# Mask products on strips of 32 rows in a clustered attention with token mixing

## The chip, the cores and the metric

The kernel runs on one core of a Trainium2 chip. The metric is the device time of one execution in microseconds, as the median of several runs of the same program; each run starts from inputs in the chip's memory and ends when the output lies there. Before the change the median of 3 runs is 792.83 us.

## The reference

Four batches, eight heads, 768 tokens and 64 channels a head. Each token of q and of k is assigned to one of 16 clusters of its head, and a query attends only to keys of its own cluster. The output of the attention goes through a token mixing stage, which the change does not touch.

```
q_assign = argmax(einsum('bhsd,hcd->bhsc', q_n, c_n)); k_assign = the same of k_n
mask   = q_assign[..., :, None] == k_assign[..., None, :]
scores = where(mask, (q @ k.T) / sqrt(D), -1e9)
attn   = softmax(scores);  x = attn @ v          # heads side by side: x is (4, 768, 512)
theta  = x @ w_theta;  zr, zi = x * cos(theta), x * sin(theta)
u      = x + w_tok_r @ zr + w_tok_i @ zi
out    = u + max(u @ w_ch, 0)
```

## The kernel before, in words

Work goes by pairs of heads: 4 batches x 4 pairs = 16 pairs. A head has 64 channels, so head j = 0 or 1 of a pair lies in rows 64j to 64j+63 of the tiles, and its products use that half of TensorE's 128 rows. Two products of different halves can run side by side; a pair of them is called a slot here.

The mask is a product too. `mk` and `mq` (128 x 768) hold per half 16 rows of one-hot cluster numbers; mk holds -2^60 wherever the key is *not* in the row's cluster. The product over these rows adds a huge negative number to a score where the clusters differ. One further row per half (row 64j+32) is 1 in mk and carries in mq the negated row maximum of a query, so that the same product also subtracts the maximum.

There are two passes over the scores, which share TensorE in the loop over units at the end of the attention part:

- *Maxima.* `max_products(u, j)` makes, for one tile of 128 queries and head j, two banks `m` of 384 keys each: a product of the high parts (hq, hk) and the mask product (mq, mk), four in all. VectorE reduces both banks to a maximum, `nm` (line 396). `shift_row` transposes the maxima (`mt`, line 404), and two DMAs (line 417) write them into the row of mq.
- *Scores.* `score_products(u, j)` makes, for 128 keys by 384 queries, one bank `sc` out of four products: hk.hq, hk.lq, lk.hq and mk.mq. ScalarE takes the exponential (`at`, line 437), GpSimd adds them up (`acc`, line 448), and `weighted` multiplies them by the values (`av`, line 509: 128 rows by 64 columns, the two heads in the two halves of the columns).

There are 192 units (16 pairs, two halves of the queries, six blocks of keys). The loop takes two units a round. The maxima run LEAD = 10 units ahead of the scores, one query tile of both heads a round. So five rounds do maxima alone, then 91 rounds do both, then five do scores alone. A round that does both issues on TensorE, in this order: scores of unit u of both heads; scores of unit u+1, head 0, beside the maxima of head 1 (`scores_beside_max`); the value products of two earlier units; scores of u+1, head 1, beside the maxima of head 0. In time, three groups of products (a head's score beside the other's maxima, both heads' scores, a head's score beside the other's maxima) therefore lie between two sets of value products. `interleave` issues the products of such a group alternately, a slot at a time. Between the groups small pieces of the next pair are put in: the assignment to clusters (`lg`, `lt`, `rt`), transposes of maxima (`mt`), sums (`sm`).

`in_order` chains the instructions of each engine in the order in which the code wrote them, so TensorE's order is that of the code. The `m` banks are four of the eight banks (two tiles of two), scores and small pieces share three, `av` has one.

The one-hot rows come about in two ways. For pair 0, `assign` compares cluster numbers with a row of 16 numbers (line 291) and transposes the result on TensorE (`ot`, line 298). For the other fifteen pairs, the cluster numbers are written to memory (`rd`) and broadcast to 16 rows per head and operand by four DMAs of 48 KB (line 326) on the SP queue; the comparison with the row number then makes mq and mk. Constants by row are `mcl` (the row's cluster number), `ncl` and `mbi` (the factor of mk by row).

Of the kernel before, what the change touches and what calls it, by code (L numbers as in the profile page):

```python
# [2 lines left out]

# [11 lines left out]
ALU = mybir.AluOpType  # L15
# [26 lines left out]
def kernel(  # L42
# [19 lines left out]
    nc = tc.nc  # L62
    B, H, D, S = qT.shape
    P = 128
    NP = H // 2
    NT = S // P
    C = cent.shape[0] // H
    DM = w_theta.shape[0]
    NCT = DM // P
    HS = S // 2  # L70
# [22 lines left out]

    mbi = cpool.tile([P, 1], F32, name="mbi")
    nc.vector.memset(mbi, 0.0)
    for r in (0, 64):
        nc.vector.memset(mbi[r:r + C], -BIG)
        nc.vector.memset(mbi[r + 32:r + 33], 1.0)

    mci = cpool.tile([P, 1], I32, name="mci")  # L100
    for r in (0, 64):
        nc.gpsimd.iota(mci[r:r + 64], pattern=[[0, 1]], base=C, channel_multiplier=-1)
    mcl = cpool.tile([P, 1], F32, name="mcl")
    nc.vector.tensor_copy(out=mcl, in_=mci)
    ncl = cpool.tile([P, 1], F32, name="ncl")
# [81 lines left out]
    for x in range(3):  # L187
        x = (NPAIR + x) % 3
# [7 lines left out]
    def m_tile(name):  # L196
        return ps0.tile([P, 2, 512], F32, tag="m", name=name)

    def bank(name):
        return ps.tile([P, 512], F32, tag="bank", name=name)  # L200
# [36 lines left out]
    def f(ap):  # L237
        return ap.bitcast(F32)

    NG = HS // C  # L240

    cl = {n: pe.tile([P, S], F32, name=f"cl{n}") for n in "qk"}

    ohp = cl["q"].bitcast(BF16).rearrange("p (n t j c) -> p n t j c", n=2, j=2, c=64)
    nc.vector.memset(ohp, 0.0)
    nc.gpsimd.memset(cl["k"], -100.0)
    wb = wc.unsqueeze(1).broadcast_to([P, NG, C])
    def assign(pi):

        b, p = divmod(pi, NP)
        raws = []
        for n, src, eng in (("q", qT, nc.sync), ("k", kT, nc.scalar if pi == 0 else nc.sync)):
            raw = pw.tile([P, S], F32, tag="raw", name=f"raw{n}{pi}", bufs=3)
            st.setdefault(pi, dict(tsets[pi % 3]))["raw" + n] = raw
            eng.dma_start(out=raw, in_=src[b, 2 * p:2 * p + 2].rearrange("h d s -> (h d) s"))
            raws.append(raw)
        yield
        lg = bank(f"lg{pi}")[:, 0:HS]  # L260
        for g in range(4):
            a, n = divmod(g, 2)
            nc.tensor.matmul(  # L263
                lg[32 * g:32 * g + 32], lhsT=cb[:, p, :, :],
                rhs=raws[n][:, a * HS:(a + 1) * HS], start=True, stop=True)
        lgs = pe.tile([P, HS], F32, tag="lgs", name=f"lgs{pi}")
        nc.scalar.copy(out=lgs, in_=lg)
        yield

        lt = (m_tile(f"lt{pi}")[:, 0] if pi > 1 else bank(f"lt{pi}"))[:, 0:HS]  # L270
        ltp = lt.rearrange("p (g a t c) -> p a g t c", a=2, t=NH, c=C)
        for t in range(HS // P):
            sl = slice(t * P, (t + 1) * P)

            nc.tensor.transpose(out=ltp[:, :, :, t], in_=lgs[:, sl], identity=identf)  # L275
        ltv = lt.rearrange("p (g c) -> p g c", c=C)
        mx = pe.tile([P, NG], F32, tag="mxl", name=f"mxl{pi}")
        nc.vector.tensor_reduce(out=mx, in_=ltv, op=ALU.max, axis=AX.X)
        eq = pe.tile([P, NG, C], BF16, tag="eq", name=f"eq{pi}")
        nc.vector.tensor_tensor(  # L280
            out=eq, in0=ltv, in1=mx.unsqueeze(2).broadcast_to([P, NG, C]), op=ALU.is_equal)
        yield

        nc.vector.tensor_tensor(out=eq, in0=eq, in1=wb, op=ALU.mult)
        rr = pe.tile([P, NG], F32, tag="rr", name=f"rr{pi}")
        nc.vector.tensor_reduce(out=rr, in_=eq, op=ALU.max, axis=AX.X)
        if pi == 0:

            keep_up(4 * WARM)
            for n in range(2):  # L290
                nc.vector.tensor_tensor(
                    out=ohp[:, n, :, :, 0:C].rearrange("p t j c -> p j t c"),
                    in0=wb.rearrange("p (n j t) c -> p n j t c", n=2, j=2)[:, n],
                    in1=rr.unsqueeze(2).broadcast_to([P, NG, C]).rearrange(
                        "p (n j t) c -> p n j t c", n=2, j=2)[:, n], op=ALU.is_equal)
                ot = bank(f"ot{n}").bitcast(BF16)[:, 0:S]
                for t in range(NT):
                    nc.tensor.transpose(
                        out=ot[:, t * P:(t + 1) * P], in_=ohp[:, n, t].rearrange("p j c -> p (j c)"), identity=identb)
                if n == 0:  # L300
                    nc.scalar.copy(out=st[pi]["mq"], in_=ot)
                else:
                    nc.vector.tensor_scalar(  # L303
                        out=st[pi]["mk"], in0=ot, scalar1=BIG, scalar2=mbi, op0=ALU.mult, op1=ALU.add)
            nc.gpsimd.memset(cl["q"], -100.0)
            return
        yield

        if "mt" in st.get(pi - 2, {}):
            mt = st[pi - 2].pop("mt")  # L310
            rt = mt[0:NG, P:2 * P]
            nc.tensor.transpose(out=rt, in_=rr, identity=identf)
            shift_out(pi - 2, 1, mt)
        else:
            rt = bank(f"rt{pi}")[0:NG, 0:P]
            nc.tensor.transpose(out=rt, in_=rr, identity=identf)
        ri = pe.tile([NG, P], F32, tag="ri", name=f"ri{pi}")
        nc.scalar.copy(out=ri, in_=rt)
        yield
        rd = dram.tile([NG, P], F32, tag="rd", name=f"rd{pi}", bufs=2)  # L320
        nc.sync.dma_start(out=rd, in_=ri)
        yield
        rv = rd.rearrange("(g t) x -> g (t x)", t=NT)
        for n, x in enumerate("qk"):
            for j in range(2):
                nc.sync.dma_start(
                    out=cl[x][64 * j:64 * j + C], in_=rv[2 * n + j:2 * n + j + 1].broadcast_to([C, S]))
        yield

        mq = st[pi]["mq"]  # L330
        if pi == 1:

            nc.gpsimd.tensor_scalar(out=mq, in0=cl["q"], scalar1=mcl, scalar2=None, op0=ALU.is_equal)
        else:
            nc.scalar.activation(out=mq, in_=cl["q"], func=AF.Abs, bias=ncl)
            yield
            nc.scalar.activation(out=mq, in_=mq, func=AF.Relu, scale=-1.0, bias=1.0)
        yield
        nc.vector.tensor_scalar(
            out=st[pi]["mk"], in0=cl["k"], scalar1=mcl, scalar2=mbi, op0=ALU.not_equal, op1=ALU.mult)  # L340
# [27 lines left out]

    def interleave(*lists):

        for x in zip(*lists):
            for j, (out, stat, cols, mov, over, start, stop) in x:
                r = slice(64 * j, 64 * j + 64)
                nc.tensor.matmul(out, lhsT=stat[r, cols], rhs=mov[r, over], start=start, stop=stop)  # L374

    def max_products(u, j):

        pi, a, i = split_u(u)
        s = st[pi]
        if i == 0 and ("nm", a) not in s:  # L380
            s["nm", a] = p2.tile([P, 2, NH], F32, tag="nm", name=f"nm{u}")
        t = a * NH + i // 2
        m = s["m", j] = m_tile(f"m{u}_{j}")
        q = slice(t * P, (t + 1) * P)
        res = []
        for c in range(2):
            k = slice(c * HS, (c + 1) * HS)
            res.append((j, (m[:, c, 0:HS], s["hq"], q, s["hk"], k, True, False)))
            res.append((j, (m[:, c, 0:HS], s["mq"], q, s["mk"], k, False, True)))
        return res  # L390

    def max_of(u, j):
# [19 lines left out]
    def shift_out(pi, a, mt):  # L412
        s = st[pi]
        mr = p2.tile([NT, P], F32R, tag="mr", name=f"mr{pi}{a}")
        nc.scalar.copy(out=mr, in_=mt[0:NT, 0:P])
        for j in range(2):
            nc.sync.dma_start(
                out=f(s["mq"][64 * j + 32:64 * j + 33, a * HS:(a + 1) * HS]).rearrange("o (t n) -> o t n", n=P),
                in_=f(mr[j * NH:(j + 1) * NH]))

    def score_products(u, j, banks=None):

        pi, a, i = split_u(u)
        s = st[pi]
        if ("at", a, i) not in s:
            s["at", a, i] = p3.tile([P, 2, HS], F32, tag="at", name=f"at{u}", bufs=NAT)
        sc = banks[:, j] if banks else ps.tile([P, 512], F32, tag="bank", name=f"sc{u}_{j}")
        sc = s["sc", j] = sc[:, 0:HS]
        k, q = slice(i * P, (i + 1) * P), slice(a * HS, (a + 1) * HS)
        parts = (("hk", "hq"), ("hk", "lq"), ("lk", "hq"), ("mk", "mq"))  # L430
        return [(j, (sc, s[x], k, s[z], q, n == 0, n == 3)) for n, (x, z) in enumerate(parts)]

    def exps(u, j):

# [236 lines left out]
    start = len(nc.cur_bb.bb.instructions)  # L671
# [30 lines left out]
    while u <= NUT or todo:  # L702
        start = len(nc.cur_bb.bb.instructions)
# [303 lines left out]
```

## Time and profile before

| | |
|---|---|
| median of 3 runs | 792.83 us (792.48 to 794.13) |
| profiled execution | 792.87 us, span 791.1 us, TensorE clock 0.991 |
| TensorE busy | 774.3 us, 98% of the span |
| VectorE, ScalarE, GpSimd busy | 572.6, 386.5, 488.3 us |
| maxima, first to last product | 14.8 to 421.8 us |
| scores, first to last product | 31.3 to 446.9 us |

Times in the profile are microseconds from the start of the span; PE is TensorE's products, PEld its weight loads, DVE VectorE, ACT ScalarE, POOL GpSimd, SPq the queue that issues DMAs. A timeline row gives start, duration, engine, line, operation, output<-operands, and the stationary tile as rows*columns; x2 or x8 is several merged. A product's duration runs over the start of the next one, since they are pipelined: the step from start to start tells what it costs. A bracket is idle time before an instruction and what ended it ("issue": nothing that the profile shows). An arrow in the waits reads "who waited <- for whom: us in total, times, longest".

### The profile page before, as it was taken

The numbers are of one execution on the slowest core, as the hardware profiler recorded it, in microseconds if no ns is written. First come the engines' busy times: TensorE is split into PE (matmuls) and PEld (weight loads), VectorE is DVE, ScalarE is ACT, GpSimd is POOL, SyncE is SP. The second block draws the span as 40 slices with busy tenths as digits, with TensorE's granted clock in tenths as the row PEclk, the third lists the DMA queues.
The fourth block names the chain that finished last, engine by engine and source line by source line (L and its number), as shares of the span: only waits on it lengthen the run. The fifth ranks groups of instructions, "written<-read, shape, count | busy, mean of one in ns | idle before, by whom it ended". The sixth has DMA issues, their size and how long they took to land.

```text
span 791.1 us, 14306 instructions
## 1 busy us (share of the span) xinstructions
PE 774.3 (98%) x5538; PEld 572.9 (72%) x5538; DVE 572.6 (72%) x688; ACT 386.5 (49%) x777; POOL 488.3 (62%) x284
## 2 busy tenths in 40 slices
PE   6999999999999999999999799999999999999998
PEld 4656665666656565656665488899889988899998
DVE  5789999999999999999989659954445433634322
ACT  3366666767676676767556436341334123403310
POOL 3388789999999999888988432561215122332131
PEclk9899999999999999999999999999999999999999
DMA  3132324332433244324343467115011411030001
GB/s 120 61 98 72 93 95 151 93 123 91 151 104 125 81 149 151 119 84 164 112 161 109 101 182 206 24 31 173 15 27 28 160 27 27 14 94 15 1 21 61
DMA packets 81583, 73.43 MB, mean 93 GB/s; under 512 B 59588, under 2 KB 65324, under 8 KB 81132
## 3 DMA queue, kind: packets, MB, share of 16 engines
q1 hardware_dynamic: 81228, 72.10, 30.5%
q8 instruction: 43, 0.70, 0.4%
q10 hardware_dynamic: 288, 0.43, 0.1%
q14 instruction: 24, 0.20, 0.1%
HBM read 57.08 MB, written 15.32 MB: 92 GB/s over the span
## 4 chain that ended last, share of the span: by engine, by line
PE 91%; DVE 5%; DMA 2%; issue 1%; SPq 1%; ACT 1%; DVEq 0%
PE y L876 26%; PE sc L374 24%; PE av L509 15%; PE tp L608 8%; PE cy L899 5%; PE m L374 4%; PE cp L899 3%; PE sm L476 2%; PE lg L263 2%; PE y L899 1%; DVE acc L452 1%; PE lt L275 1%; DVE nm L396 1%; PE mt L404 1%; DVE xl L583 1%
## 5 line engine op out<-in xcount | busy, mean ns | idle before, releaser
L437 ACT ACTIVATE at<-sc 128x384 f32<-128x384 f32 x384 | 173.6, 493 | 96.0 <-PE m L374 50.5
L396 DVE TENSOR_REDUCE nm<-m 128x1 f32<-128x768 f32 x192 | 179.6, 945 | 21.4 <-PE m L374 18.3
L448 POOL TENSOR_TENSOR acc<-at,at 128x768 f32<-128x768 f32 x64 | 129.9, 2030 | 36.0 <-ACT at L437 36.0
L374 PE MATMUL m<-hk,hq 64*128 64x384 f32 x384 | 147.1, 387 | 0.9 <-DVE nm L396 0.8
L509 PE MATMUL av<-at,vt 128*64 128x384 f32 x768 | 145.7, 499 | 1.4 <-ACT at L437 1.2
L830 POOL TENSOR_TENSOR zlc<-ab,zhc 128x512 fp32r<-128x512 f32 x24 | 32.1, 1336 | 173.2 <-ACT zhc L828 173.2
L448 POOL TENSOR_TENSOR acc<-acc,at 128x768 f32<-128x768 f32 x64 | 132.4, 2068 | 10.1 <-ACT at L437 8.0
L374 PE MATMUL m<-mk,mq 64*128 64x384 f32 x384 | 127.7, 336 | 0.8 <-DVE mk L303 0.8
L374 PE MATMUL sc<-hq,hk 64*128 64x384 f32 x384 | 116.6, 388 | 0.5 <-ACT at L437 0.5
L374 PEld LDWEIGHTS sc<-hq,hk 64*128 64x128 f32 x384 | 55.8, 184 | 62.7 <-issue 27.9
L374 PE MATMUL sc<-mq,mk 64*128 64x384 f32 x384 | 97.6, 335 | 0.0
L374 PE MATMUL sc<-hq,lk 64*128 64x384 f32 x384 | 97.3, 334 | 0.0
L374 PE MATMUL sc<-lq,hk 64*128 64x384 f32 x384 | 97.3, 334 | 0.0
L509 PEld LDWEIGHTS av<-at,vt 128*64 128x64 f32 x768 | 46.7, 136 | 60.5 <-issue 53.6
L374 PEld LDWEIGHTS m<-hk,hq 64*128 64x128 f32 x384 | 70.7, 185 | 3.4 <-DVE nm L396 2.8
L374 PEld LDWEIGHTS m<-mk,mq 64*128 64x128 f32 x384 | 71.6, 188 | 1.1 <-ACT hq L356 1.1
L613 DVE TENSOR_SCALAR kk<-tp 128x512 int32<-128x512 f32 x24 | 16.4, 683 | 77.2 <-PE tp L608 77.2
L452 DVE TENSOR_TENSOR acc<-acc,acc 128x768 f32<-128x768 f32 x30 | 70.6, 2354 | 0.0
L581 ACT CAST xh<-xT 128x512 fp32r<-128x512 f32 x23 | 14.3, 622 | 99.7 <-PE tp L608 99.7
L890 POOL TENSOR_TENSOR ul<-xT,uh 128x384 fp32r<-128x384 f32 (+1 forms) x36 | 33.5, 957 | 35.4 <-ACT uh L889 34.9
L374 PEld LDWEIGHTS sc<-lq,hk 64*128 64x128 f32 x384 | 54.9, 186 | 0.0
L374 PEld LDWEIGHTS sc<-mq,mk 64*128 64x128 f32 x384 | 54.7, 184 | 0.0
(160 smaller groups left out, 1710.3 us busy)
## 6 DMA issues: line engine op xcount, KB each, us to landing
rawq<-in_qT_dram SPq DMA_DIRECT2D x16, 384.0 KB
vt<-in_v_dram SPq DMA_DIRECT2D x16, 384.0 KB
rb<-sd SPq DMA_DIRECT2D x32, 192.0 KB
xT_d<-xt SPq DMA_DIRECT2D x16, 384.0 KB
xb<-xT_d SPq DMA_DIRECT2D x96, 64.0 KB
rawk<-in_kT_dram SPq DMA_DIRECT2D x15, 384.0 KB
w<-in_wrT_dram SPq DMA_DIRECT2D x6, 768.0 KB
w<-in_wiT_dram SPq DMA_DIRECT2D x6, 768.0 KB
```

Source lines behind the costliest of these rows:

```text
L374: nc.tensor.matmul(out, lhsT=stat[r, cols], rhs=mov[r, over], start=start, stop=stop)
L396: nc.vector.tensor_reduce(out=s["nm", a][:, j, i // 2:i // 2 + 1], in_=s["m", j][:, :, 0:HS], op=ALU.max, axis=AX.XY, negate=True)
L437: last_exp[0] = nc.scalar.activation(out=s["at", a, i][:, j], in_=s["sc", j], func=AF.Exp, scale=SCALE)
L448: last_acc[0] = nc.gpsimd.tensor_tensor(out=s["acc", a, x], in0=prev, in1=at, op=ALU.add)
L452: nc.vector.tensor_tensor(out=s["acc", a, 0], in0=s["acc", a, 0], in1=s["acc", a, 1], op=ALU.add)
L509: nc.tensor.matmul(s["av"][64 * j:64 * j + 64], lhsT=s["vt"][:, i, j, :], rhs=s["at", a, i][:, j], start=(i == 0), stop=(i == NT - 1))
L608: nc.tensor.matmul(tp, lhsT=xx[:, c, :], rhs=w_th[c][k], start=(n == 0), stop=(n == 3 * NCT - 1))
L613: nc.vector.tensor_scalar_mul(kk, tp, INV_2PI)
L830: nc.gpsimd.tensor_tensor(out=zl, in0=tr, in1=zh.bitcast(F32), op=ALU.subtract)
L876: nc.tensor.matmul(y_at(b, d, c0, c1), lhsT=zz[:, d * P:(d + 1) * P], rhs=ww[:, c0:c1], start=first and lead, stop=last, skip_group_check= ...
L890: nc.gpsimd.tensor_tensor(out=ul[:, d, :], in0=x, in1=uh[:, d, :].bitcast(F32), op=ALU.subtract)
L899: nc.tensor.matmul(cp, lhsT=w_c[d][k][:, e * P:(e + 1) * P], rhs=uu[:, d, :], start=(n == 0), stop=(n == 3 * NCT - 1), skip_group_check=True)
```

## The change

In each half of the rows, the one-hot rows are now written twice: in rows 64j to 64j+15 and in rows 64j+32 to 64j+47. A mask product then needs a strip of 32 rows instead of the half's 64. The row of the shift moves from 64j+32 to 64j+16, into the first strip. The two mask products of a query tile (one per bank `m`) take the two strips of their half and are issued one right after the other, after both products of the high parts. The mask product of a score uses the first strip of its half. The number of products stays. Setting up the second copy takes two more comparisons for pair 0, four more broadcasts for each other pair, and some constants.

```diff
@@ constants by row
     for r in (0, 64):
+        nc.vector.memset(mbi[r:r + C + 1], 1.0)
+    for r in range(0, P, 32):
         nc.vector.memset(mbi[r:r + C], -BIG)
-        nc.vector.memset(mbi[r + 32:r + 33], 1.0)
...
-    for r in (0, 64):
-        nc.gpsimd.iota(mci[r:r + 64], pattern=[[0, 1]], base=C, channel_multiplier=-1)
+    for r in range(0, P, 32):
+        nc.gpsimd.iota(mci[r:r + 32], pattern=[[0, 1]], base=C, channel_multiplier=-1)
@@ assign: pair 0, then the others
-                nc.vector.tensor_tensor(
-                    out=ohp[:, n, :, :, 0:C].rearrange("p t j c -> p j t c"),
+                for x in (0, 32):
+                    nc.vector.tensor_tensor(
+                        out=ohp[:, n, :, :, x:x + C].rearrange("p t j c -> p j t c"),
...
-                nc.sync.dma_start(
-                    out=cl[x][64 * j:64 * j + C], in_=rv[2 * n + j:2 * n + j + 1].broadcast_to([C, S]))
+                for r in (64 * j, 64 * j + 32):
+                    nc.sync.dma_start(
+                        out=cl[x][r:r + C], in_=rv[2 * n + j:2 * n + j + 1].broadcast_to([C, S]))
@@ interleave
-        for x in zip(*lists):
-            for j, (out, stat, cols, mov, over, start, stop) in x:
-                r = slice(64 * j, 64 * j + 64)
-                nc.tensor.matmul(out, lhsT=stat[r, cols], rhs=mov[r, over], start=start, stop=stop)
+        for x in zip_longest(*lists, fillvalue=()):
+            for slot in x:
+                for r, (out, stat, cols, mov, over, start, stop) in slot:
+                    nc.tensor.matmul(out, lhsT=stat[r, cols], rhs=mov[r, over], start=start, stop=stop)
+
+    def rows(j):
+        return slice(64 * j, 64 * j + 64)
+
+    def strip(j, x):
+        return slice(64 * j + 32 * x, 64 * j + 32 * x + 32)
@@ max_products
-        res = []
-        for c in range(2):
-            k = slice(c * HS, (c + 1) * HS)
-            res.append((j, (m[:, c, 0:HS], s["hq"], q, s["hk"], k, True, False)))
-            res.append((j, (m[:, c, 0:HS], s["mq"], q, s["mk"], k, False, True)))
+        k = [slice(c * HS, (c + 1) * HS) for c in range(2)]
+        res = [[(rows(j), (m[:, c, 0:HS], s["hq"], q, s["hk"], k[c], True, False))] for c in range(2)]
+        res.append([(strip(j, c), (m[:, c, 0:HS], s["mq"], q, s["mk"], k[c], False, True)) for c in range(2)])
@@ shift_out
-                out=f(s["mq"][64 * j + 32:64 * j + 33, a * HS:(a + 1) * HS]).rearrange("o (t n) -> o t n", n=P),
+                out=f(s["mq"][64 * j + C:64 * j + C + 1, a * HS:(a + 1) * HS]).rearrange("o (t n) -> o t n", n=P),
@@ score_products
-        return [(j, (sc, s[x], k, s[z], q, n == 0, n == 3)) for n, (x, z) in enumerate(parts)]
+        return [
+            [(strip(j, 0) if n == 3 else rows(j), (sc, s[x], k, s[z], q, n == 0, n == 3))]
+            for n, (x, z) in enumerate(parts)]
```

How the order moves on TensorE, in a round in the middle of the attention: the end of the two-head scores (`sc_0`, `sc_1`), then the third group (scores of head 0 beside maxima of head 1, `m_1`), up to the value products. Sizes are those of the output; the rows that a product uses are not shown. Before:

```order
L374 MATMUL sc_0_3267<-mq_156,mk_157 128x384
L374 MATMUL sc_1_3268<-mq_156,mk_157 128x384
L374 MATMUL sc_0_3280<-hq_152,hk_154 128x384
L374 MATMUL m_1_3281<-hk_154,hq_152 128x384
L374 MATMUL sc_0_3280<-lq_153,hk_154 128x384
L374 MATMUL m_1_3281<-mk_157,mq_156 128x384
L374 MATMUL sc_0_3280<-hq_152,lk_155 128x384
L374 MATMUL m_1_3281<-hk_154,hq_152 128x384
L374 MATMUL sc_0_3280<-mq_156,mk_157 128x384
L374 MATMUL m_1_3281<-mk_157,mq_156 128x384
L509 MATMUL av_3168<-at_3207,vt_2781 64x384 x2
```

After, at the same place:

```order
L379 MATMUL sc_0_3667<-mq_169,mk_170 128x384
L379 MATMUL sc_1_3668<-mq_169,mk_170 128x384
L379 MATMUL sc_0_3680<-hq_165,hk_167 128x384
L379 MATMUL m_1_3681<-hk_167,hq_165 128x384
L379 MATMUL sc_0_3680<-lq_166,hk_167 128x384
L379 MATMUL m_1_3681<-hk_167,hq_165 128x384
L379 MATMUL sc_0_3680<-hq_165,lk_168 128x384
L379 MATMUL m_1_3681<-mk_170,mq_169 128x384 x2
L379 MATMUL sc_0_3680<-mq_169,mk_170 128x384
L520 MATMUL av_3568<-at_3607,vt_3177 64x384 x2
```

The maxima's mask products (`mk`, `mq`) stood second and fourth of their list; now both stand together as its third entry, and the score's mask product comes last with no partner. Rows with `mq` and `mk` are those that now use 32 rows; all others use 64, and the value products 128.

On the SP queue, around the broadcasts for one pair (`clq` and `clk` are the cluster numbers of q and k, `rd` the copy in memory, `rawq` and `rawk` the next pair's inputs). Before:

```order
L321 DMA rd_1588<-ri_1586 24x128
L326 DMA clq<-rd_1588 16x768 x2
L326 DMA clk<-rd_1588 16x768 x2
L257 DMA rawq_1608<-in_qT_dram 128x768
L257 DMA rawk_1610<-in_kT_dram 128x768
```

After:

```order
L325 DMA rd_1610<-ri_1608 24x128
L331 DMA clq<-rd_1610 16x768 x4
L331 DMA clk<-rd_1610 16x768 x4
L260 DMA rawq_1634<-in_qT_dram 128x768
L260 DMA rawk_1636<-in_kT_dram 128x768
```

Each pair has eight broadcasts in place of four, ahead of the same loads. ScalarE's order is the same in both programs; VectorE has two more comparisons for pair 0, and nothing else moves behind them.

More of the change, by code (lines that the diff above doesn't have):

```diff
@@ L2 @@
 from contextlib import ExitStack, nullcontext
+from itertools import zip_longest
 import concourse.bass as bass
@@ L290, in assign @@
             for n in range(2):
-                nc.vector.tensor_tensor(
-                    out=ohp[:, n, :, :, 0:C].rearrange("p t j c -> p j t c"),
-                    in0=wb.rearrange("p (n j t) c -> p n j t c", n=2, j=2)[:, n],
-                    in1=rr.unsqueeze(2).broadcast_to([P, NG, C]).rearrange(
-                        "p (n j t) c -> p n j t c", n=2, j=2)[:, n], op=ALU.is_equal)
+                for x in (0, 32):
+                    nc.vector.tensor_tensor(
+                        out=ohp[:, n, :, :, x:x + C].rearrange("p t j c -> p j t c"),
+                        in0=wb.rearrange("p (n j t) c -> p n j t c", n=2, j=2)[:, n],
+                        in1=rr.unsqueeze(2).broadcast_to([P, NG, C]).rearrange(
+                            "p (n j t) c -> p n j t c", n=2, j=2)[:, n], op=ALU.is_equal)
                 ot = bank(f"ot{n}").bitcast(BF16)[:, 0:S]
```

## The prediction

> **What bounds the kernel now.** I read the page's first part, then the busy time of the stage that the change touches, then the TensorE timeline of one round of the unit loop. The chip's own record of this execution is 792.87 us (span 791.1), 0.04 us over the median of the three runs, so the sum is made against 792.9.
>
> ```profile
> PE 774.3 (98%) x5538; PEld 572.9 (72%) x5538; DVE 572.6 (72%) x688; ACT 386.5 (49%) x777; POOL 488.3 (62%) x284
> PE 91%; DVE 5%; DMA 2%; issue 1%; SPq 1%; ACT 1%; DVEq 0%
> 31.00:422.00 391.00, 390.39 (x3211) 239.54 (x3209) 368.52 (x356) 256.57 (x547) 355.15 (x171) 1.00 0.36 116
> L374 PE MATMUL sc<-hq,hk x384: 327/395/608, 31.3 to 446.3; 64*128 64x384 f32 x192
> L374 PE MATMUL m<-mk,mq x384: 327/333/522, 16.1 to 421.8; 64*128 64x384 f32 x192
> L396 DVE TENSOR_REDUCE nm<-m x192: 886/946/959, 16.9 to 422.2; 128x1 f32<-128x768 f32 x192
> ```
>
> The first two lines are the page's busy times and the chain that ended last: TensorE carries 91% of it. The third is the busy time from 31 to 422 us (PE, PEld, DVE, ACT, POOL, then clock): TensorE never rests, DVE is at 94% (368.5 of 391), GpSimd at 91%. The last three date the stage. A product with the maxima runs from 16.1 to 421.8 and a score product from 31.3 to 446.3; 192 reductions are 96 query tiles of two heads. The loop runs ten units ahead by two, so 5 rounds do maxima alone, 91 do both (31.3 to 421.8, 4.29 us each) and 5 do scores alone.
>
> One round, on TensorE: start, duration, output<-operands, rows*columns of the stationary tile. Here x2 are the two heads side by side.
>
> ```profile
> 203.15 0.44 PE L374 MATMUL sc<-hq,hk 64*128 64x384 f32 x1
> 203.16 0.44 PE L374 MATMUL m<-hk,hq 64*128 64x384 f32 x1
> 203.43 0.33 PE L374 MATMUL sc<-lq,hk 64*128 64x384 f32 x1
> ...
> 203.96 0.33 PE L374 MATMUL sc<-hq,hk 64*128 64x384 f32 x2
> 204.13 0.33 PE L374 MATMUL sc<-lq,hk 64*128 64x384 f32 x2
> 204.30 0.34 PE L374 MATMUL sc<-hq,lk 64*128 64x384 f32 x2
> 204.48 0.34 PE L374 MATMUL sc<-mq,mk 64*128 64x384 f32 x2
> 204.69 0.44 PE L374 MATMUL sc<-hq,hk 64*128 64x384 f32 x1
> 204.70 0.44 PE L374 MATMUL m<-hk,hq 64*128 64x384 f32 x1
> 204.97 0.33 PE L374 MATMUL sc<-lq,hk 64*128 64x384 f32 x1
> ...
> 205.32 0.34 PE L374 MATMUL sc<-mq,mk 64*128 64x384 f32 x1
> 205.32 0.34 PE L374 MATMUL m<-mk,mq 64*128 64x384 f32 x1
> 205.59 1.51 PE L509 MATMUL av<-at,vt 128*64 128x384 f32 x8
> 207.03 0.27 PE L404 MATMUL mt<-identf,nm 128*6 128x128 f32 x1
> 207.23 0.51 PE L263 MATMUL lg<-rawq,cb 128*32 128x384 f32 x1
> ...
> 207.25 0.51 PE L263 MATMUL lg<-rawk,cb 128*32 128x384 f32 x1
> ```
>
> The two halves of the rows work side by side: sc and m start 0.01 us apart. One slot (a product in each half) takes 0.175 us: six from 203.43 to 204.48. A round has three groups of four slots. Two steps are longer. The last slot before the value products (av, another tile shape) takes 0.27 (205.32 to 205.59), and the first slot after them takes 0.28 (203.15 to 203.43). The weight loads tell why:
>
> ```profile
> 203.15 0.18 PEld L374 LDWEIGHTS sc<-hq,hk 64*128 64x128 f32 x1 [0.60 <-issue]
> 203.26 0.19 PEld L374 LDWEIGHTS sc<-lq,hk 64*128 64x128 f32 x1
> 205.59 0.20 PEld L509 LDWEIGHTS av<-at,vt 128*64 128x64 f32 x4 [0.25 <-issue]
> 211.90 0.55 PE L275 MATMUL lt<-identf,lgs 128*128 128x128 f32 x3
> 212.38 0.44 PE L374 MATMUL sc<-hq,hk 64*128 64x384 f32 x1
> 212.66 0.34 PE L374 MATMUL sc<-lq,hk 64*128 64x384 f32 x1
> ```
>
> Within one shape the load for the 203.43 product starts at 203.26, under the product before it. At a change of shape it starts with its own product (203.15 and 203.15), after an idle stretch that waits for nothing the profile names. So a change costs 0.27 - 0.175 = 0.095 us until the array is empty, and 0.28 - 0.175 = 0.105 us of open weight load: 0.20 us. The last three rows are a change in which the 128 columns stay and only the rows go from 128 to 64: the three transposes end at 212.45 by the record, the last began at 212.18 (0.27 long, as mt above), the next shape starts 0.20 later, and its first step is again 0.28. The change from 128*6 to 128*32 (207.03 to 207.23) is a step of 0.20 too. Every kind of change that I found in the stage pays.
>
> **The change, part by part.**
>
> *The slots.* The maxima lose one slot in a half of the rows, but each group pairs them with four score products, and the fourth (the score's mask product) stays. In the code's order a group is now: 64-row sc with m; 64-row sc with m; 64-row sc; then two m and one sc on strips of 32 rows. With the two heads' scores it is three 64-row slots and one of 32 rows. So if shapes don't mix, each group still has four slots and nothing is gained. An earlier finish of one half could be used by the next group only if 32-row and 64-row products can share the array.
>
> *The shape changes.* Now a round has two (into 64 rows, out to av). After the change it has seven: in, three times 64 to 32, twice 32 to 64, and out. Five more at 0.20 us are 1.00 us a round, 91 us in 91 rounds. No row of this trace shows 64*128 against 32*128. The bounds are below: zero if the two sizes share the array; 0.095 each (43 us) if only the emptying is paid and weights are loaded ahead; 0.20 each as in all rows above. I take 0.20, since the row nearest in kind (only rows change, 212.38) pays both parts.
>
> By the Trainium skill, "TensorEngine Tiling (Array Packing)", Key Properties, changing the tiling mode, not merely the tile, drains TensorE, and 64x128 and 32x128 stand there as different modes. For the shapes in this trace the 0.20 us steps agree; for 32 rows no row here shows it. By it the sum is the one taken here; without it, the first rival's.
>
> *What the longer round hides.* In the quoted round the third group starts late: 204.48 to 204.69 is 0.21, not 0.175, and its first step is 0.28, so 0.14 us a round goes to a score bank whose exponential is not done.
>
> ```profile
> PEld sc L374 <- ACT at L437: 15.6, 74, 0.8
> ```
>
> The wait arises since the bank of the first group's scores is wanted again five slots later. With the shape changes between, that is 0.6 us later, and the wait should go: minus 15.6 us (ends 0 and 15.6). DVE (94%) and GpSimd (91%) get slack with every microsecond that TensorE loses, so nothing else becomes late. 91.0 - 15.6 = 75.4.
>
> *Rounds with scores alone.* Eight slots and two changes become eight slots and five changes, 5 x 3 x 0.20 = 3.0 us at most.
>
> ```profile
> 432.39 0.34 PE L374 MATMUL sc<-hq,hk 64*128 64x384 f32 x1
> 433.19 0.44 PE L374 MATMUL sc<-hq,hk 64*128 64x384 f32 x1 [0.46 <-ACT at L437]
> L396 DVE TENSOR_REDUCE nm<-m 128x1 f32<-128x768 f32 x14 | 13.0, 952 | 5.5 <-PE m L374 5.5
> ```
>
> One such round already has TensorE idle 0.46 us for ACT, which swallows some: between 0 and 3.0, I take 1.5.
>
> *Rounds with maxima alone.* Each head's four slots become three with a change of shape between: a head takes 0.28 + 0.27 + 0.375 and then the next shape, about 0.4 us more per tile, 2.0 us in five. The reductions behind them (0.95 us each, 13 us busy, 5.5 us waiting for m) set much of this stretch: between 0 and 2.0, I take 1.0.
>
> *Start-up.* The first pair's one-hot comparison is written twice, and lies on the way to the first mask.
>
> ```profile
> L291 DVE TENSOR_TENSOR clq<-wc,rr x2: 351/354/357, 13.1 to 13.4; 128x192 bf16<-128x192 bf16 x2
> L303 DVE TENSOR_SCALAR mk<-ot,mbi 128x768 fp32r<-128x768 bf16 x1 | 1.0, 1017 | 1.2 <-PE ot L298 1.2
> ```
>
> Two more at 0.354 us are 0.7 us; the second pair of comparisons partly lies beside the first six transposes, and mk already waits 1.2 us for those. Between 0.35 and 0.7, I take 0.4. The memsets and iotas on columns of one element are hidden by the loads of the first inputs.
>
> *DMAs.* Fifteen pairs get four more broadcasts of 48 KB: 60, 2.9 MB of 73, on engines with a mean share of 0.36.
>
> ```profile
> L326 SPq DMA_DIRECT2D clq<-rd x30: 308/333/1362, 25.1 to 381.0; - x30
> L326 SPq DMA_DIRECT2D clk<-rd x30: 370/418/1518, 25.9 to 381.9; - x30
> POOL mq L333: 6.7, 1
> ```
>
> SP issues for 2 x 0.33 + 2 x 0.42 = 1.5 us more in each pair (25 us long in six rounds); the next pair's raw loads queue behind that and are wanted rounds later. The only waiter is GpSimd in pair 1, 0.7 us later; its next work needs exponentials that start after 31 us. Nothing: the cover is that slack, and gone it would be 0.7 once.
>
> Sum: 91.0 - 15.6 + 1.5 + 1.0 + 0.4 = 78.3; 792.9 + 78.3 = 871 us. With every term at its end for full changes (nothing hidden, 3.0, 2.0, 0.7) it is 890; with 0.18 a change and the low ends it is 859. That is the likeliest case's own range.
>
> **The rivals.**
>
> *Strips share the array with halves (faster).* If what makes the array wait is two products wanting the same rows, not different shapes, the fourth score product of a half runs beside the first product of the next group, and a round has eleven slots: 91 x 0.175 = 16 us less. DVE's 368.5 busy us of 391 allow up to 22, so it would fit: about 778 (777 to 785 with start-up and a late bank). For it speaks that halves run 0.01 us apart and that four column strips do too (lg, 207.23 to 207.25); against it, that each change of shape in the rows costs 0.20. It decides at the 64-to-32 step: under about 0.03 us a change (0.14 to 0.17 hidden per round, over five) nothing is lost.
>
> The Trainium skill, "TensorE: Matmul & The Clock Gate", Part 3, speaks for this rival, as far as it goes: products on different 32-row strips run at once, four of them 3.07 times as fast as in turn. It doesn't say so of mixed sizes, and no run here shows 32 rows.
>
> *Emptying without open weight loads.* 32-row weights are loaded ahead: 43 - 15.6 + 2.9 = 30, 823 us. Against it stands 212.38 to 212.66.
>
> *Three strips not at once.* If the two m and the sc of 32 rows take two slots, two groups a round are 0.175 longer: 91 x 0.35 = 32 more, 903 us. Against it: lg's four column strips start together.
>
> *It doesn't matter (same).* The halves' gain equals start-up and waits, within 0.2% (1.6 us, about what these runs tell from no change): DVE at 94% and the score banks would have to set the pace, but TensorE waits for them only 0.17 us a round.
>
> **The numbers.** Full changes of shape 0.70, emptying alone 0.08, strips in turn 0.07, sharing 0.12, no matter 0.03. Predicted 871. A range from 822 to 904 holds the first three, 0.85, and leaves out 0.15; the likeliest alone would be 859 to 890. Faster 0.12, same 0.03, slower 0.85.
>
> **What would show it.** In the timeline the m mask products read 32*128 and start together with the score's, 0.27 after the last 64-row product, and the next 64-row product follows 0.37 later; a round takes 5.1 us instead of 4.29; idle weight-load time put down to issue grows by more than 30 us while the wait for ACT's exponentials goes; DVE's share in the stage falls to about 80%. I am wrong if a 32-row and a 64-row product of different halves are seen at once, or if the 64-to-32 step is 0.175.

## The result, and the profile after

The changed kernel takes 872.3 us (median of 4 runs, 870.63 to 875.98) against 792.65 before: 1.101 times as long, 95% interval 1.097 to 1.1049. The prediction was 871 in a range of 822 to 904. The profiled execution took 872.31 us, its span 870.5.

First the busy times and the chain that ended last, then the dates of the products at the line that is now 379 (engine, operation, count, durations in ns, first and last start).

```profile
PE 856.9 (98%) x5538; PEld 569.3 (65%) x5538; DVE 587.7 (68%) x692; ACT 391.6 (45%) x777; POOL 470.1 (54%) x286
PE 88%; DVE 5%; DMA 3%; ACT 2%; issue 1%; SPq 1%; POOL 0%; DVEq 0%; ACTq 0%
L379 PE MATMUL m<-hk,hq x384: 328/437/687, 16.1 to 502.5; 64*128 64x384 f32 x192
L379 PE MATMUL m<-mk,mq x384: 433/436/684, 17.4 to 502.9; 32*128 32x384 f32 x192
L379 PE MATMUL sc<-hq,hk x384: 435/440/687, 39.7 to 528.4; 64*128 64x384 f32 x192
L379 PE MATMUL sc<-mq,mk x384: 433/434/439, 40.7 to 529.1; 32*128 32x384 f32 x192
39.70:502.90 463.20, 463.00 (x3207) 234.41 (x3203) 385.83 (x355) 261.20 (x547) 337.11 (x171) 1.00 0.34 104
```

TensorE does the same 5538 products and is busy 83 us longer, while its weight loads are not. The mask products have 32 rows, and their records run over 0.43 us, as only the first products after a change of shape did before: each contains an open weight load. In the stage that does both passes (last row) VectorE has fallen from 94% to 83% (385.8 of 463.2). By these dates the 79.4 us between the two spans lie as follows.

| stretch | before | after | difference |
|---|---|---|---|
| start to the first product of the maxima | 14.8 | 16.1 | +1.3 |
| maxima alone, to the first score | 16.5 | 23.6 | +7.1 |
| 91 rounds with both, to the last maximum | 390.5 | 463.2 | +72.7 |
| scores alone, to the last one | 25.1 | 26.2 | +1.1 |
| the rest | 344.2 | 341.4 | -2.8 |

One round on TensorE, in the same columns as before the change:

```profile
222.71 0.44 PE L379 MATMUL sc<-hq,hk 64*128 64x384 f32 x1
222.71 0.44 PE L379 MATMUL m<-hk,hq 64*128 64x384 f32 x1
222.99 0.33 PE L379 MATMUL sc<-lq,hk 64*128 64x384 f32 x1
222.99 0.34 PE L379 MATMUL m<-hk,hq 64*128 64x384 f32 x1
223.16 0.34 PE L379 MATMUL sc<-hq,lk 64*128 64x384 f32 x1
223.43 0.44 PE L379 MATMUL m<-mk,mq 32*128 32x384 f32 x2
223.43 0.44 PE L379 MATMUL sc<-mq,mk 32*128 32x384 f32 x1
223.80 0.44 PE L379 MATMUL sc<-hq,hk 64*128 64x384 f32 x2
224.08 0.34 PE L379 MATMUL sc<-lq,hk 64*128 64x384 f32 x2
...
224.52 0.44 PE L379 MATMUL sc<-mq,mk 32*128 32x384 f32 x2
224.89 0.44 PE L379 MATMUL sc<-hq,hk 64*128 64x384 f32 x1
...
225.61 0.44 PE L379 MATMUL m<-mk,mq 32*128 32x384 f32 x2
...
225.98 0.54 PE L520 MATMUL av<-at,vt 128*64 128x384 f32 x2
223.43 0.18 PEld L379 LDWEIGHTS m<-mk,mq 32*128 32x128 f32 x2 [0.25 <-issue]
223.80 0.19 PEld L379 LDWEIGHTS sc<-hq,hk 64*128 64x128 f32 x2 [0.18 <-issue]
```

Read the starts: 0.28, 0.17, then 0.27 to the strips, then 0.37 to the next 64-row product, three times over: 222.71 to 225.98 is 3.27 us, the figure worked out for it. The strips do run side by side (the three of 223.43 start together), but a 64-row product of the other half does not run with them: at 223.16 one half works alone and the other waits. The weight loads of the last two rows start with their own products, after an idle stretch that waits for nothing the profile names. That is the full price, at each change into the strips and out of them. Over the whole program, the idle time of the score products' weight loads that is put down to issue grows from 27.9 to 81.6 us, and their wait for ScalarE's exponentials falls from 15.6 to 0.5 us, as the prediction's signs had it.

The rule of the Trainium skill that the prediction weighed ("TensorEngine Tiling (Array Packing)", Key Properties: a change of tiling mode drains the array) holds here for 64x128 and 32x128. The last 64-row step ahead of the strips takes 0.27 us instead of 0.175; the strips' own step takes 0.37, since the open weight load and the next change both lie in it.

### The profile page after: what moved, and what is told of

It is laid out like the page before. It is cut to its first block, busy times and chain, and to the rows that moved or that the text cites. A ratio compares the mean times of both kernels' runs of the same rounds, so it can differ in the third digit from the quotient of the medians.

```text
span 870.5 us, 14427 instructions
## 1 busy us (share of the span) xinstructions
PE 856.9 (98%) x5538; PEld 569.3 (65%) x5538; DVE 587.7 (68%) x692; ACT 391.6 (45%) x777; POOL 470.1 (54%) x286
## 4 chain that ended last, share of the span: by engine, by line
PE 88%; DVE 5%; DMA 3%; ACT 2%; issue 1%; SPq 1%; POOL 0%; DVEq 0%; ACTq 0%
PE sc L379 27%; PE y L887 18%; PE av L520 16%; PE m L379 10%; PE tp L619 5%; PE cy L910 4%; PE cp L910 2%; PE lg L266 2%; PE sm L487 1%; PE y L910 1%; PE lt L278 1%; DMA rb<-sd 1%; PE mt L413 1%; DMA wtmp<-in_w_ch_dram 1%; DMA xT_d<-xt 1%
## 5 line engine op out<-in xcount | busy, mean ns | idle before, releaser
L459 POOL TENSOR_TENSOR acc<-acc,at 128x768 f32<-128x768 f32 x64 | 122.8, 1919 | 33.4 <-ACT at L448 31.5
L379 PE MATMUL sc<-hq,hk 64*128 64x384 f32 x384 | 125.7, 440 | 0.3 <-ACT at L448 0.3
L379 PE MATMUL sc<-mq,mk 32*128 32x384 f32 x384 | 123.7, 435 | 0.0
L379 PE MATMUL m<-hk,hq 64*128 64x384 f32 x384 | 122.2, 398 | 0.2 <-DVE nm L405 0.2
L379 PE MATMUL m<-mk,mq 32*128 32x384 f32 x384 | 87.1, 449 | 0.3 <-DVE mk L307 0.3
L379 PEld LDWEIGHTS m<-mk,mq 32*128 32x128 f32 x384 | 36.4, 186 | 49.9 <-issue 49.1
L379 PEld LDWEIGHTS sc<-mq,mk 32*128 32x128 f32 x384 | 51.6, 181 | 25.0 <-issue 24.7
L463 DVE TENSOR_TENSOR acc<-acc,acc 128x768 f32<-128x768 f32 x30 | 65.3, 2176 | 0.0
L379 PEld LDWEIGHTS m<-hk,hq 64*128 64x128 f32 x384 | 58.6, 191 | 4.5 <-issue 3.4
L379 PEld LDWEIGHTS sc<-hq,lk 64*128 64x128 f32 x384 | 52.9, 185 | 0.0
```

The source lines that it names most:

```text
L459: last_acc[0] = nc.gpsimd.tensor_tensor(out=s["acc", a, x], in0=prev, in1=at, op=ALU.add)
L463: nc.vector.tensor_tensor(out=s["acc", a, 0], in0=s["acc", a, 0], in1=s["acc", a, 1], op=ALU.add)
```

## The experiments

Theory A: five more changes of shape in a round, 0.20 us each, cost the time. Rivals: the second copies with their broadcasts; the order of the products; a price for each 32-row slot whatever stands next to it; and, for the gain that was hoped for, that a slot saved in one half would have been worth 16 us without the changes of shape.

**All mask products over 64 rows again.**

```diff
-        res.append([(strip(j, c), (m[:, c, 0:HS], s["mq"], q, s["mk"], k[c], False, True)) for c in range(2)])
+        res += [[(rows(j), (m[:, c, 0:HS], s["mq"], q, s["mk"], k[c], False, True))] for c in range(2)]
-            [(strip(j, 0) if n == 3 else rows(j), (sc, s[x], k, s[z], q, n == 0, n == 3))]
+            [(rows(j), (sc, s[x], k, s[z], q, n == 0, n == 3))]
```

> The changed kernel, with its order of products, second copies, broadcasts and start-up, but every mask product over its half's 64 rows, so that no 32-row product is left and a group has four slots again. If the changes of shape between 64 and 32 rows cost the time (five more in a round, 0.20 us each), a round falls from 5.08 back to 4.29 us, and the whole to 793 to 796 us (the later start-up of about 1.3 us stays). If the second copies, the broadcasts or the new order of the maxima's products cost it, it stays above 860 us.

799.12 us, 1.0088 of before (1.0058 to 1.0118). 73 of the 80 us go with the 32-row products alone (those in the rounds with maxima alone included); second copies, broadcasts, order and start-up are all still in it. But it is 3 us above what I expected, and 7 above before. From the waits between 40 and 430 us, and the dates:

```profile
L379 PE MATMUL sc<-hq,hk x384: 327/415/687, 34.4 to 454.3; 64*128 64x384 f32 x192
PEld lg L266 <- DMA rawk<-in_kT_dram: 2.6, 4, 1.0
PEld sc L379 <- ACT at L448: 14.3, 71, 0.6
```

Four times TensorE waits for the next pair's raw inputs, a wait that the kernel before does not have; the score bank's wait is back.

**Which part of the rest costs these 7 us.** Two kernels. The first is the kernel before with the maxima's two mask products after both products of the high parts:

```diff
             res.append((j, (m[:, c, 0:HS], s["hq"], q, s["hk"], k, True, False)))
+        for c in range(2):
+            k = slice(c * HS, (c + 1) * HS)
             res.append((j, (m[:, c, 0:HS], s["mq"], q, s["mk"], k, False, True)))
```

> The kernel before, with the maxima's products in the changed order (both of the high parts, then both mask products), all over 64 rows and without second copies, broadcasts or new start-up. The run with all mask products over 64 rows was 6 us slower than before and showed raw inputs coming late behind the broadcasts. If the second copies with their broadcasts and start-up cost those 6 us, this one equals the kernel before within 0.3%: 791 to 795 us. If the order of the products costs it, it is 797 to 800 us.

792.3 us, 1.0008 (0.999 to 1.0027): the order is free. The second is the run with 64 rows throughout, without the second broadcasts:

```diff
-                for r in (64 * j, 64 * j + 32):
+                for r in (64 * j,):
                     nc.sync.dma_start(
```

> The run with all mask products over 64 rows, without the second broadcasts: fifteen pairs have four broadcasts again, and only the first pair has second copies. What is left of the change is the order of the products and the start-up (two more comparisons, constants, and a small reduction that now stands behind a large subtraction on VectorE: about 1.3 us). If the broadcasts ahead of the raw inputs on the SP queue cost the rest of that run's 6 us, this is 793 to 795 us. If start-up and the clock in the first rounds cost it, it stays at 797 to 800 us.

793.95 us, 1.0024 (1.0012 to 1.0036), inside the first case. So start-up leaves about 2 us, and the broadcasts about 5 (799.1 to 794.0). TensorE's wait for raw inputs goes with them: at full speed the loads that stand behind four more broadcasts come late. That named wait is only 2.9 us in all, though. By the dates of the two traces the scores begin 2.1 us earlier without the second broadcasts (32.3 instead of 34.4 us) and run 4.9 us shorter (415.0 instead of 419.9 us from the first to the last), of which 2.2 are given back behind the last one. The rest of the 5 us is not traced, nor whether the number of issues or the bytes delay the loads.

**Two changes of shape, and nothing else.** Into the kernel before, one small product per head goes ahead of the two heads' scores; in one kernel over 64 rows, in the other over 32.

```diff
+    def probe(u, j, n):
+        pi, a, i = split_u(u)
+        s = st[pi]
+        r = slice(64 * j, 64 * j + n)
+        nc.tensor.matmul(s["sc", j][:, 0:P], lhsT=s["hk"][r, i * P:(i + 1) * P],
+                         rhs=s["hq"][r, a * HS:a * HS + P], start=True, stop=True)
```

> The kernel before with one small product more per head ahead of the two heads' scores in each round (hk by 128 columns of hq, into the bank that the first score product then overwrites), over the half's 64 rows: no change of shape. It is the base for the run beside it. The added slot is some 0.11 us (bounded by a weight load), but the round has 0.16 us of waiting for a score bank (0.92 us from a score's mask product to the bank's next use), which the added slot fills: 0 to 2 us in all, 792 to 796 us. If TensorE had no such wait, 91 x 0.11 = 10 us: 803 us.

> The same, with the small products over the first 32 rows of their half: the same instructions in the same order, one size of rows apart, so two changes of shape more per round and nothing else. At 0.20 us a change (emptying and open weight load) a round becomes 2.73 us between value products instead of 2.44: 27 us over 91 rounds and about 2 in the last five, 820 to 825 us. If only the emptying (0.095) is paid, the rounds become 2.57 and it is 805 to 808 us. If 32 and 64 rows share the array, it equals the run beside it.

793.44 us, 1.0029 (1.0008 to 1.0049), and 818.37 us, 1.0338 (1.0315 to 1.036). The same program with the same order, 25 us apart by the number of rows, a little less than the 27 to 29 that I worked out. In one round of each, from value products to value products, it is 0.29 us (213.92 to 216.67 over 32 rows, 203.22 to 205.68 over 64), where two whole changes would be 0.40; the score bank's wait hides part of that, and the remainder is not worked out. Emptying alone is excluded: I had put it at 12 to 15 us, and with nothing hidden it would be 19 (0.19 us at 101 places). In the run over 32 rows:

```profile
214.55 0.33 PE L375 MATMUL m<-mk,mq 64*128 64x384 f32 x1
214.82 0.33 PE L460 MATMUL sc<-hq,hk 32*128 32x128 f32 x2
215.08 0.44 PE L375 MATMUL sc<-hq,hk 64*128 64x384 f32 x2
215.36 0.34 PE L375 MATMUL sc<-lq,hk 64*128 64x384 f32 x2
```

The small 32-row product of 128 columns takes 0.26 from start to next start, and the steps beside it are 0.27 and 0.28. The run over 64 rows shows the other side: the added pair costs 1.6 us over all rounds, not 10. That fits a round that waits for a score bank anyway.

**Only the maxima on strips.** The score's mask product goes back to 64 rows.

```diff
-            [(strip(j, 0) if n == 3 else rows(j), (sc, s[x], k, s[z], q, n == 0, n == 3))]
+            [(rows(j), (sc, s[x], k, s[z], q, n == 0, n == 3))]
```

> The changed kernel, but the score's mask product goes over 64 rows; only the maxima's two are on strips. A round then has two 32-row slots in place of three, but still four changes of shape more than the kernel before, and one product that stands alone ahead of the value products. By 0.20 us a change its products take 0.28+0.17+0.27, 0.37, 0.28+5x0.17+0.27, 0.37, 0.37 = 3.24 us between two sets of value products, 3.27 in the changed kernel, and perhaps 0.1 to 0.2 more for a score bank that comes late: 868 to 885 us. If the price hangs on the number of 32-row slots (0.81 us over three in a round), one fewer makes it about 24 us faster: 846 to 850 us.

898.37 us, 1.1351 (1.1318 to 1.1385): with fewer 32-row slots it is 26 us slower than the changed kernel. That settles the rival (a price per 32-row slot would have made it faster), but it is also outside my own 868 to 885. Where the count failed, from its timeline:

```profile
222.00 0.44 PE L379 MATMUL m<-mk,mq 32*128 32x384 f32 x2
222.37 0.44 PE L379 MATMUL sc<-mq,mk 64*128 64x384 f32 x1
222.38 0.61 PE L379 MATMUL sc<-hq,hk 64*128 64x384 f32 x2
...
223.01 0.51 PE L379 MATMUL sc<-mq,mk 64*128 64x384 f32 x2
223.40 0.44 PE L379 MATMUL sc<-hq,hk 64*128 64x384 f32 x1
223.40 0.44 PE L379 MATMUL m<-hk,hq 64*128 64x384 f32 x1
```

The lone score product of 222.37 does run beside the next group's first (222.38). I had let that half keep its lead into the third group. But the third group's first score wants a bank whose exponential comes later, at 223.40, 1.03 us after that score's mask product started with an open weight load, and both halves start it together. Lead lost (0.175), wait and open weight load (about 0.15): 3.57 us between value products (221.28 to 224.85) and not 3.24.

**Three slots of one shape.** The maxima's second mask product is left out, all others use 64 rows.

```diff
-        res = [[(rows(j), (m[:, c, 0:HS], s["hq"], q, s["hk"], k[c], True, False))] for c in range(2)]
+        res = [[(rows(j), (m[:, c, 0:HS], s["hq"], q, s["hk"], k[c], True, c == 1))] for c in range(2)]
-        res.append([(strip(j, c), (m[:, c, 0:HS], s["mq"], q, s["mk"], k[c], False, True)) for c in range(2)])
+        res.append([(rows(j), (m[:, 0, 0:HS], s["mq"], q, s["mk"], k[0], False, True))])
```

> As the run with all mask products over 64 rows, but the maxima's second mask product is left out (so the second bank's maximum is that of unmasked scores): a query tile's maxima then truly take three slots, all of one shape. If halves of equal shape let a finished half go on into the next group, a round has eleven slots, 0.175 us less: 91 x 0.175 = 16 us, 777 to 781 us. If VectorE (94% busy) or the score banks set the pace by then, the gain is under 5 us: 788 to 794 us.

800.68 us, 1.0123 (1.0091 to 1.0155), outside both of my ranges: its base is the run with four slots of the same shape, which took 799.1 and not 793 to 796. Against that base the slot was truly saved, and nothing was gained:

```profile
211.87 0.44 PE L379 MATMUL sc<-hq,hk 64*128 64x384 f32 x1
...
212.51 0.33 PE L379 MATMUL sc<-mq,mk 64*128 64x384 f32 x1
212.52 0.50 PE L379 MATMUL sc<-hq,hk 64*128 64x384 f32 x2
...
213.04 0.52 PE L379 MATMUL sc<-mq,mk 64*128 64x384 f32 x2
213.43 0.44 PE L379 MATMUL sc<-hq,hk 64*128 64x384 f32 x1
213.43 0.44 PE L379 MATMUL m<-hk,hq 64*128 64x384 f32 x1
...
214.32 0.54 PE L520 MATMUL av<-at,vt 128*64 128x384 f32 x2
```

The score's last product (212.51) and the next group's first (212.52) run side by side, so a half has a slot's lead. Then the third group waits: 213.43 is 0.92 us after 212.51. In the kernel before that distance is the same: for the bank's mask product that starts with 203.78, the next use is at 204.69, 0.91. It is the time from a score's last product over its exponential (0.49 us) to the bank's next use, with three banks for scores, and it holds whether four or five slots lie between. After it both halves begin together and the lead is gone: 211.87 to 214.32 is 2.45 us, as in the kernel before (203.15 to 205.59, 2.44). So in these rounds the score banks give back what the slot saved. That the banks hold the pace is read from these distances and from the probe above; no run had a fourth bank, since all eight are taken. VectorE, the other limit that I had named, is not excluded in this run: it is busy for 381.1 of the 397.5 us of the stage (96%, against 93% in the run with four slots), and weight loads of TensorE wait 11.0 us for its reductions between 40 and 430 us, against 4.3 us there.

**The rounds with maxima alone.**

```diff
+        if wide:
+            return [res[0], [(rows(j), (m[:, 0, 0:HS], s["mq"], q, s["mk"], k[0], False, True))],
+                    res[1], [(rows(j), (m[:, 1, 0:HS], s["mq"], q, s["mk"], k[1], False, True))]]
...
-                interleave(max_products(ahead, j))
+                interleave(max_products(ahead, j, True))
```

> The changed kernel, but the five rounds that do maxima alone use 64-row mask products in the old order. In the changed kernel these rounds ran with steps of 0.32 us where the others take 0.175, and scores began at 39.7 us, not 31.3. If the changes of shape in these rounds keep TensorE's clock down, scores begin at 32 to 34 us and the whole falls by 5 to 8 us, to 864 to 867 us. If start-up or the broadcasts delay them, it stays within 2 us of the changed kernel's 872.

865.98 us, 1.0943 of before (1.0902 to 1.0983), 6.3 us under the changed kernel; scores begin at 33.1 us. Both lie where the first case had them. The clock in this stretch, four microseconds a row (its column is the one before the DMA share): first the run with only the maxima on strips, whose first rounds are those of the changed kernel, then this one. The changed kernel's own record shows no change of clock there, though its steps are as long.

```profile
20.00:24.00 4.00, 4.00 (x16) 1.57 (x8) 0.96 (x1) 0.48 (x1) 1.91 (x2) 0.50 0.53 172
32.00:36.00 4.00, 4.00 (x16) 2.21 (x15) 1.84 (x3) 0.26 (x1) 0.85 (x1) 0.50 0.39 98
20.00:24.00 4.00, 3.74 (x28) 2.84 (x25) 2.47 (x4) 0.48 (x1) 1.80 (x2) 0.89 0.49 165
24.00:28.00 4.00, 2.79 (x17) 1.77 (x16) 3.73 (x6) 0.26 (x1) 0.00 (x0) 0.96 0.01 3
28.00:32.00 4.00, 4.00 (x27) 2.70 (x29) 2.29 (x4) 0.26 (x1) 0.92 (x1) 0.50 0.46 98
```

With strips TensorE is busy all the time by the record and gets half its clock throughout. With 64 rows the clock comes back at about 21 us and stays up while TensorE is idle for 1.21 of 4 us (0.96, 17 products), but then it falls here too (0.50, 27 products). So strips in these rounds hold the clock down for longer. They did not bring it down: from 17 to 18 us it falls in both runs (0.68 and 0.72 in that microsecond). What decides it is not shown; the number of products in a row does not tell by itself.

Half a clock alone does not cost 6 us either. A tile of both heads at half clock, first in the changed kernel, then in this run (the `idle` product ends the tile; the first row's x2 are two banks of one head, the fourth's x2 are the two heads):

```profile
21.73 1.01 PE L379 MATMUL m<-hk,hq 64*128 64x384 f32 x2
22.67 0.69 PE L379 MATMUL m<-mk,mq 32*128 32x384 f32 x2
23.29 1.00 PE L379 MATMUL m<-hk,hq 64*128 64x384 f32 x2
...
24.84 0.82 PE L213 MATMUL idle<-identb 128*128 128x128 bf16 x6
29.23 0.84 PE L379 MATMUL m<-hk,hq 64*128 64x384 f32 x2
...
30.96 0.82 PE L213 MATMUL idle<-identb 128*128 128x128 bf16 x6
```

With 64 rows the two heads run side by side, and the tile takes 1.73 us. With strips the second head's 64-row products wait until the first head's strips are through, and it takes 3.11 us. A slot is 0.32 us at this clock and a change 0.30 (1.56 us for a head, less three slots, is two changes). Strips and the clock together make TensorE the bound of these rounds; no run has strips at full clock there.

**More filler in those rounds of the kernel before.** In the kernel before the clock fell between 24 and 31 us as well, which points to a faster version of it: more small products to keep it up, twice as many and, in a second kernel, three times (`3 * WARM`).

```diff
-            keep_up(WARM)
+            keep_up(2 * WARM)
```

> The kernel before, with twelve in place of six small filler products after each of the rounds that do maxima alone. There, steps went to 0.32 us from 24 to 31 us in the kernel before. If the filler keeps the clock up, scores begin up to 2 us earlier and the whole is 0.1 to 0.3% faster, 790 to 792 us; if the clock falls anyway, the filler itself costs 1 to 4 us, 794 to 797 us.

> The kernel before with eighteen small filler products after each of the rounds of maxima alone (twelve made it 0.16% faster, and its clock stayed full from 20 to 32 us). If the clock needs no more than twelve, the six added cost 0.05 us each where TensorE is behind: 790 to 793 us. If runs differ in whether twelve suffice, eighteen is steadier: 788.5 to 790.5 us.

790.21 us, 0.9984 (0.997 to 0.9998), and 792.02, 1.0001 (0.9988 to 1.0015). With twelve the clock stayed full from 16 to 32 us and scores began at 29.7 instead of 31.3; with eighteen the clock stays full too, but scores begin at 30.5 and the time is that of before. Twelve has the lowest median of all kernels here, by 0.16%, at the edge of what can be told. The fastest executions of the kernel before (788.5 us) are as fast as those with twelve (788.9). The difference is that with twelve none took 792 to 794 us.

## Why the prediction was right, point by point

- *The slots.* Right: a group still has four, and the strips start together.
- *The shape changes, 0.20 us each.* Right: 0.27 into the strips and 0.37 from them in the profile, 0.27 and 0.26 in the probe, whose products are shorter. The rivals "emptying alone", "strips in turn" and "sharing" are each excluded by one row of the round after the change.
- *What the longer round hides.* Right: 15.6 us were to be absorbed. 91 rounds grew by 72.7 where 75.4 was forecast. The quoted rounds alone (2.44 to 3.27 us) would give 75.5, so the missing 2.8 us lie in other rounds; where isn't shown.
- *Rounds with maxima alone: 1.0 taken, 7.1 measured.* This is the step that failed. I took the reductions for the cover, TensorE at full clock, and the heads one after the other in both kernels. The strips went with half a clock from start to end of the stretch (a slot 0.32 us, a change 0.30), the two heads no longer ran side by side (3.11 us a tile, where 64 rows at half clock take 1.73), and TensorE became the bound. Its quoted upper end, 2.0, was too low too; the falling clock between 24 and 31 us stood in the profile before.
- *Start-up: 0.4 taken, 1.3 measured.* The comparisons cost what was said. Missed was a swap in VectorE's order: the reduction of the centroids' squares, ahead of a large subtraction on VectorE before, stands behind it now. Rows of before, then of after:

```profile
4.63 0.22 DVE L218 TENSOR_REDUCE cs<-csq 128x1 f32<-128x64 f32 x1
5.07 0.96 DVE L360 TENSOR_TENSOR lq<-rawq,hq 128x768 fp32r<-128x768 f32 x1 [0.21 <-ACT hq L356]
5.06 0.96 DVE L365 TENSOR_TENSOR lq<-rawq,hq 128x768 fp32r<-128x768 f32 x1 [0.89 <-ACT hq L361]
5.93 0.21 DVE L221 TENSOR_REDUCE cs<-csq 128x1 f32<-128x64 f32 x1
```

  The chain of the cluster assignment hangs on it, 0.9 us later. The statement that nothing moves on VectorE behind the comparisons was wrong by this one row.
- *DMAs: nothing.* In the changed kernel no row has TensorE waiting for raw inputs. That its longer rounds cover them fits this, but no run took the second broadcasts out of it. At full speed they cost 5 us; "wanted rounds later" did not hold for the raw inputs.
- *Scores alone: 1.5 taken, 1.1 measured.*
- *The rest: 0 taken, -2.8 measured.* Nearly all of this is the clock of the two profiled executions, at the seam to the token mixing. The same sixteen products, before and after:

```profile
452.88 2.79 PE L476 MATMUL sm<-acc,ecol 128*32 128x384 f32 x16 [2.46 <-DVE xt L522]
533.91 1.50 PE L487 MATMUL sm<-acc,ecol 128*32 128x384 f32 x16 [2.46 <-DVE xt L533]
```

  The next products start 2.71 us later before (455.59) and 1.43 us later after (535.34), and eight products further on it is 5.94 and 3.37 us (458.82, 537.28), 2.6 us apart; the clock granted in the 10 us behind the last score is 0.73 before and 1.00 after. The run with the new order, which has the speed of before and no strips, has no such dip either: its sixteen products take 1.42 us (452.16 to 453.58), its rest 341.9. So this term is no effect of the strips.
- *The sum.* That it came out within 1.3 us is luck: 6.1 and 0.9 too little in the rounds with maxima alone and at the start, against 2.7, 0.4 and 2.8 too much elsewhere. The large term, the changes of shape, is not luck.
- *The rival that ended faster.* Its price was wrong as well as its mechanism: a slot saved in each half is worth nothing here, as the run with three slots of one shape shows.

## What to carry to other kernels

Before packing small products side by side, count how often the shape of the stationary tile changes, and price a change from the trace: the last step before it less the usual step, plus the first step after it less the usual one (here 0.095 + 0.105 us, more than a whole slot of 0.175). A saved slot pays only if the next thing that TensorE waits for has room: look for the wait at the head of the following group (here a score bank, 0.92 us after its last product) and test it by adding a slot, which costs little where a bank holds the pace (1.6 us of 10 here). A cost can hide under a slowdown, as the broadcasts seem to here, and shows only once the slowdown is taken out.

## What the runs showed of the hardware that I had not expected

Three products on three strips start within 0.01 us of each other, yet a 64-row product in the other half of the array waits for them. In the run with only the maxima on strips, the other half is free at 222.00, and the 64-row product there starts at 222.37, when the strips are through. So here the size had to be the same; free rows were not enough.

TensorE stayed at half its clock for about 20 us while its record was 100% busy (4.00 of 4.00 us, clock 0.50), and came up only in the rounds with scores after it. The kernel before did so too, for 6 us (25 to 31). The Trainium skill ("TensorE: Matmul & The Clock Gate", Part 1) has the clock released by some 3.4 us of sustained activity; the runs here agree only if activity is something else than the busy time of the record; what counts as activity they do not show.
